# Attention with a soft mixture of experts: all transposes of an iteration in one run, and query loads of one iteration each

## The chip, the cores and the metric

The kernel runs on one core of a Trainium2 chip. The core has five engines with queues of their own: TensorE (PE; its weight loads are listed as PEld), VectorE (DVE), ScalarE (ACT), GpSimd (POOL) and SyncE (SP), which here only issues loads and stores; 16 DMA engines move the data. The metric is the device time of one execution in microseconds. Before the change three runs took 406.70, 407.28 and 407.36 us, median 407.28.

## The reference, cut to what matters

Three blocks follow one another, all in float32:

```
# attention: batch 4, 8 heads, 512 local and 32 global tokens, head size 64
s_g  = scale * q_g @ [k_g, k_l].T           ; out_g = softmax(s_g) @ [v_g, v_l]
s_l  = scale * q_l @ [k_g, k_l].T           # local keys only where |i - j| <= 32
out_l = softmax(s_l) @ [v_g, v_l]
x = [out_g, out_l] as 2176 x 512            # tokens of all batches, heads side by side
# soft mixture of 8 experts with 4 slots each
logits = x @ phi                            # 2176 x 32
d = softmax over the tokens ; slot_in = d.T @ x
slot_out = relu(slot_in @ w1[e]) @ w2[e]
y = softmax over the slots(logits) @ slot_out
# last block
h = y @ w_in ; out = (h - tanh(h)) @ w_out
```

## The kernel before, in words

The attention is a loop over `it` from 0 to 32. Iteration `it` handles block `it` of 32: a set s = it // 4 of one batch's four heads, and a quarter t = it % 4 of its tokens. It is software-pipelined: in iteration `it` the kernel computes the scores of block `it`, transposes the probabilities of block `it` - 1 and multiplies those of block `it` - 2 with v. Behind it, chains of small steps turn finished blocks into the input of the mixture. Engines work their queues in the order in which the code lists the instructions; waits between engines come from the data that they share. A tile of a pool with one buffer waits for the last reader of the tile before it.

In one iteration the steps that the change and the prediction speak of are listed in this order:

- `open_chains` (L625): the first half of each chain's present step (copies out of PSUM, exponentials), on ACT and DVE.
- `local_scores` (L236): TensorE's scores "sc" (L248) from the spread query `q_b[2]` and the keys, VectorE's masking (L254), ScalarE's exponentials (L258).
- `roll_k` (L218) and `spread_q(it + 1)` (L138) on GpSimd; both are copies by `pcopy` (L210). The spread overwrites the one `q_b[2]` tile, so it waits for the scores of this iteration, and the next scores wait for it.
- `local_transpose(it - 1)` (L265): four transposes "ptp" (L269) and a copy on ScalarE.
- `win_head` (L616) in every second iteration from 4 to 18: ScalarE's first step of turning float64 words of w_in into float32; the later steps run on VectorE in the next iteration.
- `local_values(it - 2)` (L274): "X" (L281); `global_values(it - 2)` (L467): "xgp" (L475), when t of that block is 0 or 1; `roll_v(it - 2)` (L223) on GpSimd, when t is 0, 1 or 2.
- `step_chains` (L630): the second half of each chain's step, in the order in which the chains were appended, all on TensorE. Among them are the transposes `turn_x` (L307, "xTp" L311, four), the two `turn` steps of `global_probs` (L449 four, L457 two), `turn` of `global_turn` (L494, one) and `turn` of `dispatch` (L379, one), and also steps that aren't transposes, `logits` (L339) and `gather` (L387).
- `global_probs` (L416) when it % 4 is 2: "gsc" (L430); then on GpSimd `spread_k` (L123) when t is 1 and `spread_v` (L127) when t is 3.
- SyncE: `load_q` (L132) in every second iteration, for the two blocks `it` + 4 and `it` + 5; loads of v when t is 2 or 3; then weights, as many KB as a pace (L724) allows; `load_qk` when t is 3. A load waits for the last reader of the place that it fills; that of a query waits for `spread_q(it + 1)`.

PSUM has eight banks: two for scores, one each for ptp, X, xgp and psL, two for psM. Before, psM held gsc, both turns of the global probabilities, xTp and the chains of `dispatch`, and psL held only the one transpose of `global_turn`.

After the loop (from L827) come the last X, the last logits, then the experts' weights (L971, L1010) and the last block.

Of the kernel before, what the change touches and what calls it, by code (L numbers as in the profile page):

```python
# [8 lines left out]
F32 = mybir.dt.float32  # L9
# [53 lines left out]
def band_attention_soft_moe_tanhshrink_kernel(  # L63
# [138 lines left out]
    NG = 4 * NST  # L202
# [103 lines left out]

    def turn_x(i):  # L307
        def transpose():
            ps = psM.tile([128, 512], F32, tag="m", name="xTp")
            for kc in range(4):  # L310
                T.transpose(ps[:, 128 * kc:128 * kc + 128], x_cols(i, 128 * kc, 128), ident)  # L311
            if i % 2 == 0:
                x2 = wk.tile([128, 2, 512], F32, tag="xT", name="xT", bufs=2)
                xT_t[i], xT_t[i + 1] = x2[:, 0, :], x2[:, 1, :]
            S.copy(out=xT_t[i], in_=ps)

        return [(None, transpose)]

# [6 lines left out]
    def dispatch(b, lbank=psm, tbank=psm, gbank=psm):  # L327
# [4 lines left out]
        st = {}  # L332
# [71 lines left out]
                    out=a, in0=a, scalar=f[rows], in1=st["s", cols.start][rows, cols], op0=ALU.mult, op1=ALU.add  # L404
                )

        chain = [(None, logits), (exps, turn), (turn_out, gather), (add, None)]
        return chain, dict(
            start=start, logits=logits, maxima=maxima, powers=powers, sums=sums, keep=keep, turn=turn,
            turn_out=turn_out, gather=gather, add=add,  # L410
# [5 lines left out]
    def global_probs(s):  # L416
        k, st = k_t[s], {}
        cuts = ((0, 512), (512, 576))

        def scores():  # L420
            for lo, hi in cuts:
                st[lo] = psM.tile([128, hi - lo], F32, tag="m", name="gsc")
            for lo, c, n, planes, groups in (
                (0, 0, 480, slice(0, 3), slice(0, 5)), (0, 480, 32, 3, 0), (512, 0, 64, slice(0, 2), 5),
            ):
                for i in range(2):
                    kn = k[:, i, planes, groups]
                    if n == 480:
                        kn = kn.rearrange("p q g c -> p g q c")
                    T.matmul(  # L430
                        st[lo][64 * i:64 * i + 64, c:c + n], lhsT=qg_t[s][:, 64 * i:64 * i + 64],
                        rhs=kn, skip_group_check=True, tile_position=(0, 64 * i),
                    )

        def exps():
            a = wk.tile([128, 4], F32, tag="gst", name="gst")
            for i, (lo, hi) in enumerate(cuts):
                V.tensor_reduce(out=a[:, i:i + 1], in_=st[lo], op=ALU.max, axis=AX.X)
            V.tensor_scalar(
                out=a[:, 2:3], in0=a[:, 0:1], scalar1=a[:, 1:2], scalar2=-0.125, op0=ALU.max, op1=ALU.mult  # L440
            )
            for o, i in (
                (pgl[:, 0:5, 0:96], st[0][:, 0:480].rearrange("p (i c) -> p i c", i=5)),
                (pgl[:, 0, 96:128], st[0][:, 480:512]),
                (pgl[:, 5, 0:64], st[512]),
            ):
                S.activation(out=o, in_=i, func=AF.Exp, scale=0.125, bias=a[:, 2:3])

        def turn():  # L449
            st["t"] = psM.tile([128, 512], F32, tag="m", name="gtp")  # L450
            for i in range(4):
                T.transpose(st["t"][:, 128 * i:128 * i + 128], pgl[:, i, :], ident)

        def turn_out():
            S.copy(out=gpt[:, 0:4].rearrange("p i c -> p (i c)"), in_=st["t"])

        def turn2():  # L457
            st["u"] = psM.tile([128, 256], F32, tag="m", name="gtp2")
            for i in range(2):
                T.transpose(st["u"][:, 128 * i:128 * i + 128], pgl[:, 4 + i, :], ident)  # L460

        def turn2_out():
            S.copy(out=gpt[:, 4:6].rearrange("p i c -> p (i c)"), in_=st["u"])

        return [(None, scores), (exps, None), (None, turn), (turn_out, turn2), (turn2_out, None)]

    def global_values(g):  # L467
        s, t = divmod(g, 4)
# [22 lines left out]
    def global_turn(b):  # L491
        st = {}

        def turn():  # L494
            st["p"] = psL.tile([128, 128], F32, tag="l", name="gxp")
            T.transpose(st["p"], gx_t.pop(b), ident)

        def turn_out():
            S.copy(out=xgT[:, :, b, :], in_=st["p"].rearrange("p (j q) -> p j q", j=4))

        return [(None, turn), (turn_out, None)]


    cool = []
# [120 lines left out]
    def open_chains():  # L625
        for c in chains:
            if c[0][0]:
                c[0][0]()

    def step_chains():  # L630
        for c in chains:
            if c[0][1]:
                c[0][1]()
        chains[:] = [c[1:] for c in chains if len(c) > 1]


# [3 lines left out]
    with tc.manual_schedule():  # L640
# [23 lines left out]
        for it in range(NG + 1):  # L664
# [8 lines left out]
                        spread_q(it + 1, (pcopy, pcopy))  # L673
            if 1 <= it < NG + 1:
                local_transpose(it - 1)
            free.extend(cool)
            cool.clear()
            if it < NG and it >= C0 and (it - C0) % 2 == 0 and (it - C0) // 2 < NIN:
# [7 lines left out]
                roll_v(it - 2)  # L686
            for f in last:
                f()
            step_chains()
            gs = (it + 2) // 4 if it % 4 == 2 and it + 2 < NG else 0 if it == 0 else None  # L690
            if gs is not None:
                c = global_probs(gs)
# [10 lines left out]
            i = it - 2  # L703
# [7 lines left out]
                spread_v(0)  # L711
            if it < NG and t == 3 and s < NST - 1:
                spread_v(s + 1)
            if it % 2 == 0 and it < NG - 4:
                load_q(it // 2 + 2)
            if it < NG:
                if it == NG - 5:
                    phi_g = ap_.tile([128, 192], F32, tag="qg", name="phi_g", bufs=1)
# [107 lines left out]

        dg["start"]()  # L827
        open_chains()
        values_last()
        step_chains()  # L830
        dg["logits"]()
        dg["maxima"]()
        last_turn(0)
# [670 lines left out]
```

## Time and profile before

| what | value |
|---|---|
| three runs | 406.70, 407.28, 407.36 us |
| the profiled execution's own time | 406.85 us |
| its span, first to last instruction | 405.1 us |
| mean granted TensorE clock | 0.993 of full speed |
| TensorE busy in the span | 382.9 us (95%) |
| VectorE, ScalarE, GpSimd busy | 276.2, 218.2, 209.7 us |
| bytes moved | 70.43 MB |
| the chain that ended last | PE 76%, issue 6%, POOL 5%, DVE 4%, DMA 3% |

"Busy" is the time in which an engine works on an instruction; matmuls are pipelined and overlap, so start-to-start distances say more of TensorE than durations do. In an answer of the trace, "[0.39 <-POOL q L210]" behind a row says that the engine stood idle for 0.39 us before it and what ended the idle time; "issue" means that the trace shows nothing that it waited for. One float32 matmul of the kernel gives several records, so the counts (x16, x32) are larger than the code's.

### The profile page before, as it was taken

To read this page: it belongs to the slowest core of one execution; us is meant where nothing else is said; L and a number is where in the kernel's file an instruction comes from. 1 tells how busy PE (TensorE), PEld (TensorE's weight loads), DVE (VectorE), ACT (ScalarE), POOL (GpSimd) and SP (SyncE) were. 2 spreads that over 40 slices of the span, in tenths; PEclk is the share of its full clock that TensorE was granted. 3 is DMA by queue.
4 is the path that set the end of the run, shared out by engine and by line. 5 is a ranking of instruction groups with operands and counts; after the bars stand their busy time and mean duration, and the time that the engine had idled before them with its cause. 6 is when DMAs were issued, how large, how long until landed. Compare 5 with 4: busy or idle time off the path is not lost.

```text
span 405.1 us, 10230 instructions
## 1 busy us (share of the span) xinstructions
PE 382.9 (95%) x3767; PEld 279.6 (69%) x3767; DVE 276.2 (68%) x833; ACT 218.2 (54%) x542; POOL 209.7 (52%) x275
## 2 busy tenths in 40 slices
PE   7889889989999899999999999999989999999994
PEld 3677667766787433336877786786868888888873
DVE  4577698766476526449998886787879997555541
ACT  2677666865766202248655645566575645345330
POOL 3676576665564010016866444455575668347441
PEclk9999999999999999999999999999999999999998
DMA  6899999999768989999303101003100003002104
GB/s 182 264 401 317 321 335 268 357 334 294 266 183 270 332 254 418 416 420 385 111 0 105 53 1 53 0 4 94 60 2 2 0 28 129 0 2 113 44 2 138
DMA packets 33834, 70.43 MB, mean 174 GB/s; under 512 B 3824, under 2 KB 10736, under 8 KB 33776
## 3 DMA queue, kind: packets, MB, share of 16 engines
q1 hardware_dynamic: 33632, 69.56, 50.3%
q8 instruction: 32, 0.52, 0.5%
q14 instruction: 26, 0.21, 0.2%
q10 hardware_dynamic: 144, 0.13, 0.1%
HBM read 65.22 MB, written 4.46 MB: 172 GB/s over the span
## 4 chain that ended last, share of the span: by engine, by line
PE 76%; issue 6%; POOL 5%; DVE 4%; DMA 3%; ACT 3%; SPq 2%; DVEq 0%; POOLq 0%
PE a L1175 13%; PE a L1176 13%; PE a L1174 13%; PE sc L248 7%; PE a L971 4%; PE a L1010 4%; PE h L1133 4%; PE X L281 3%; PE ptp L269 3%; SPq L104 2%; PE gsc L430 2%; POOL q L210 2%; PE xTp L311 2%; PE ps L344 1%; DVE slot L1150 1%
## 5 line engine op out<-in xcount | busy, mean ns | idle before, releaser
L1161 POOL TENSOR_TENSOR slot<-slot 128x384 fp32r<-128x384 f32 x96 | 98.7, 1031 | 83.5 <-ACT slot L1157 79.8
L1174 PE MATMUL a<-slot 128*128 128x512 f32 x272 | 106.9, 393 | 1.3 <-ACT v_w L1182 0.7
L1176 PE MATMUL a<-slot 128*128 128x512 f32 x272 | 107.8, 396 | 0.0
L1175 PE MATMUL a<-slot 128*128 128x512 f32 x272 | 107.5, 395 | 0.0
L1146 DVE SCALAR_TENSOR_TENSOR h<-slot,h 128x384 f32<-128x384 f32 x96 | 51.5, 537 | 38.7 <-ACT slot L1140 38.4
L1157 ACT CAST slot<-slot 128x384 fp32r<-128x384 f32 x96 | 47.6, 496 | 49.5 <-DVE slot L1150 49.0
L1140 ACT ACTIVATE slot<-h 128x384 f32<-128x384 f32 x96 | 45.3, 473 | 34.5 <-PE h L1133 33.9
L1174 PEld LDWEIGHTS a<-slot 128*128 128x128 f32 x272 | 51.1, 188 | 14.2 <-ACT v_w L1182 1.5
L1176 PEld LDWEIGHTS a<-slot 128*128 128x128 f32 x272 | 51.0, 188 | 11.4
L1175 PEld LDWEIGHTS a<-slot 128*128 128x128 f32 x272 | 51.0, 188 | 9.3 <-POOL slot L1037 1.0
L1150 DVE TENSOR_TENSOR slot<-slot,h 128x384 f32<-128x384 f32 x96 | 50.8, 529 | 8.0 <-DVE h L1146 0.5
L258 ACT ACTIVATE sm<-sm,mb 128x128 f32<-128x128 f32 x128 | 41.2, 396 | 15.5 <-DVE mb L254 15.2
L248 PE MATMUL sc<-k,q 128*64 128x128 f32 x512 | 39.0, 294 | 4.9 <-POOL q L210 3.8
L210 POOL TENSOR_SCALAR v<-v 32x1300 f32<-32x1300 f32 (+5 forms) x40 | 34.2, 855 | 13.9 <-PE xgp L475 11.4
L248 PEld LDWEIGHTS sc<-k,q 128*64 128x64 f32 x512 | 33.3, 208 | 11.1 <-POOL q L210 5.9
L210 POOL TENSOR_SCALAR q<-q 64x256 f32<-64x256 f32 x62 | 27.5, 444 | 20.5 <-issue 11.0
L254 DVE CUSTOM_DVE_ANT_0 sm<-sc,mask 128x128 f32<-128x128 f32 x128 | 30.2, 284 | 10.9 <-PE sc L248 9.7
L1037 POOL TENSOR_TENSOR slot<-k_w,slot 128x512 fp32r<-128x512 f32 x16 | 20.7, 1296 | 32.5 <-ACT slot L1036 32.3
L1133 PE MATMUL h<-slot 128*128 128x384 f32 x96 | 32.4, 339 | 0.8 <-DVE slot L1150 0.6
L1133 PEld LDWEIGHTS h<-slot 128*128 128x128 f32 x96 | 17.9, 188 | 12.0 <-DVE slot L1150 5.9
L281 PE MATMUL X<-v,pt 128*32 128x65 f32 x1024 | 22.1, 223 | 1.4 <-issue 1.4
L281 PEld LDWEIGHTS X<-v,pt 128*32 128x32 f32 x1024 | 16.5, 109 | 7.2 <-issue 6.1
(239 smaller groups left out, 526.2 us busy)
## 6 DMA issues: line engine op xcount, KB each, us to landing
slot<-in_w_dram SPq DMA_DIRECT2D x55, 512.0 KB, 7.6
slot<-in_w_out_dram SPq DMA_DIRECT2D x9, 512.0 KB, 4.8
slot<-in_w_in_dram SPq DMA_DIRECT2D x16, 256.0 KB, 6.5
k<-in_k_dram SPq DMA_DIRECT2D x7, 576.0 KB, 7.8
q<-in_q_dram SPq DMA_DIRECT2D x15, 256.0 KB, 5.4
out_dram<-o SPq DMA_DIRECT2D x15, 256.0 KB, 2.1
slot<-in_w_in_dram SPq DMA_DIRECT2D x7, 512.0 KB, 10.0
v<-in_v_dram SPq DMA_DIRECT2D x8, 390.0 KB, 5.5
```

The costliest lines, as they stand in the source:

```text
L210: G.tensor_scalar(out=o, in0=i, scalar1=0.0, scalar2=1.0, op0=ALU.add, op1=ALU.mult)
L248: T.matmul(sc[64 * i:64 * i + 64, a, :], lhsT=q_b[2][:, 256 * i + jj:256 * i + 256:4], rhs=k[:, i, :, WINDOWS[t][jj][0]], skip_group_check ...
L281: T.matmul(X[32 * jj:32 * jj + 32, h, :], lhsT=pt[:, 128 * jj + 32 * h:128 * jj + 32 * h + 32], rhs=v[:, WINDOWS[t][jj][0], 65 * h:65 * h ...
L1133: T.matmul(h, lhsT=mst(128 * fc, 128), rhs=cst(128 * t0 + c.start, n))
L1140: S.activation(out=u, in_=h, func=AF.Square)
L1146: V.scalar_tensor_tensor(out=h, in0=u, scalar=-2.5, in1=h, op0=ALU.add, op1=ALU.mult)
L1150: V.tensor_tensor(out=g, in0=u, in1=h, op=ALU.mult)
L1157: S.copy(out=ghi, in_=g)
L1161: G.tensor_tensor(out=glo, in0=g, in1=ghi.bitcast(F32), op=ALU.subtract)
L1174: T.matmul(acc_t[j], lhsT=ghi[:, c], rhs=whi[fc], start=first, stop=False)
L1175: T.matmul(acc_t[j], lhsT=ghi[:, c], rhs=wlo[fc], start=False, stop=False)
L1176: T.matmul(acc_t[j], lhsT=glo[:, c], rhs=whi[fc], start=False, stop=last)
```

## The change

All steps that are transposes get a third element "T" in their chain. `step_chains` takes an argument and runs twice per iteration: right behind `local_transpose` for the steps with "T", and at its old place for the others; only the second call advances the chains. The x transposes use psL (the one of tile 14 uses psM), and `global_turn` uses psM. `load_q` is called in every iteration, for block `it` + 5 alone (in iteration 0 for blocks 4 and 5), with 128 columns instead of 256.

```diff
     def turn_x(i):
         def transpose():
-            ps = psM.tile([128, 512], F32, tag="m", name="xTp")
+            pool, tag = (psM, "m") if i == 14 else (psL, "l")
+            ps = pool.tile([128, 512], F32, tag=tag, name="xTp")
...
-        return [(None, transpose)]
+        return [(None, transpose, "T")]
...
-        chain = [(None, logits), (exps, turn), (turn_out, gather), (add, None)]
+        chain = [(None, logits), (exps, turn, "T"), (turn_out, gather), (add, None)]
...
-        return [(None, scores), (exps, None), (None, turn), (turn_out, turn2), (turn2_out, None)]
+        return [(None, scores), (exps, None), (None, turn, "T"), (turn_out, turn2, "T"), (turn2_out, None)]
...
         def turn():
-            st["p"] = psL.tile([128, 128], F32, tag="l", name="gxp")
+            st["p"] = psM.tile([128, 128], F32, tag="m", name="gxp")
...
-        return [(None, turn), (turn_out, None)]
+        return [(None, turn, "T"), (turn_out, None)]
...
-    def step_chains():
+    def step_chains(turns):
         for c in chains:
-            if c[0][1]:
+            if c[0][1] and (len(c[0]) > 2) == turns:
                 c[0][1]()
+        if turns:
+            return
         chains[:] = [c[1:] for c in chains if len(c) > 1]
...
                 local_transpose(it - 1)
+            step_chains(True)
             free.extend(cool)
...
-            step_chains()
+            step_chains(False)
...
-            if it % 2 == 0 and it < NG - 4:
-                load_q(it // 2 + 2)
+            for g in (4, 5) if it == 0 else (it + 5,):
+                if g < NG:
+                    load_q(g // 2, slice(128 * (g % 2), 128 * (g % 2) + 128))
...
         open_chains()
+        step_chains(True)
         values_last()
-        step_chains()
+        step_chains(False)
```

## Rows read from the trace of the kernel before

**Rows 1.** Windows: busy us (and instructions) of each engine, granted clock, DMA share, GB/s.
```profile
core 0: us, PE busy (x) PEld busy (x) DVE busy (x) ACT busy (x) POOL busy (x), PEclk, DMA share, GB/s
20.00:100.00 80.00, 72.62 (x1558) 56.92 (x1548) 59.39 (x293) 55.44 (x158) 52.69 (x94) 1.00 0.99 328
100.00:124.00 24.00, 23.09 (x518) 18.61 (x520) 14.05 (x88) 17.78 (x52) 14.71 (x30) 1.00 0.73 236
140.00:160.00 20.00, 19.85 (x162) 6.29 (x161) 8.99 (x38) 2.23 (x7) 1.90 (x2) 0.91 0.92 325
```

**Rows 2.** Waits of TensorE, 8 to 132 us: total us, times, longest.
```profile
PE sc L248 <- POOL q L210: 3.8, 8, 1.0
```

**Rows 3.** TensorE's timeline, starts of scores: start us, us, instruction, idle before.
```profile
70.73 1.23 PE L248 MATMUL sc<-k,q 128*64 128x128 f32 x16 [0.39 <-POOL q L210]
...
81.71 1.23 PE L248 MATMUL sc<-k,q 128*64 128x128 f32 x16 [0.48 <-POOL q L210]
...
102.94 1.23 PE L248 MATMUL sc<-k,q 128*64 128x128 f32 x16
```

**Rows 4.** TensorE's timeline, stops without a releaser, first and last of seven.
```profile
20.83 0.32 PE L475 MATMUL xgp<-v,pg 128*32 128x65 f32 x7 [0.30 <-issue]
...
106.31 0.33 PE L460 MATMUL gtp<-ident,pg 128*128 128x128 f32 x1 [0.69 <-issue]
```

**Rows 5.** TensorE's timeline, groups in iterations 16 and 26.
```profile
68.55 0.67 PE L281 MATMUL X<-v,pt 128*32 128x65 f32 x32
69.14 0.66 PE L452 MATMUL gtp<-ident,pg 128*128 128x128 f32 x4
69.64 0.27 PE L496 MATMUL gxp<-ident,gx 128*128 128x128 f32 x1
69.75 0.60 PE L311 MATMUL xTp<-ident,x 128*128 128x128 f32 x4
...
108.16 0.66 PE L269 MATMUL ptp<-ident,sm 128*128 128x128 f32 x4
108.75 0.67 PE L281 MATMUL X<-v,pt 128*32 128x65 f32 x32
109.23 0.63 PE L475 MATMUL xgp<-v,pg 128*32 128x65 f32 x32
```

**Rows 6.** GpSimd's timeline, iterations 7, 10, 15 and 16, and 24.
```profile
36.19 1.63 POOL L210 TENSOR_SCALAR v<-v 32x1300 f32<-32x1300 f32 x1 [0.20 <-DMA v<-in_v_dram]
...
44.02 0.88 POOL L210 TENSOR_SCALAR q<-q 64x256 f32<-64x256 f32 x2
...
66.36 2.67 POOL L210 TENSOR_SCALAR v<-v 32x260 f32<-32x260 f32 x3 [0.39 <-PE xgp L475]
...
69.80 0.88 POOL L210 TENSOR_SCALAR q<-q 64x256 f32<-64x256 f32 x2
...
101.66 0.88 POOL L210 TENSOR_SCALAR q<-q 64x256 f32<-64x256 f32 x2
```

**Rows 7.** SyncE's timeline around the query load of iteration 10.
```profile
40.89 0.55 SPq L104 DMA_DIRECT2D slot<-in_w_dram  x1
44.92 0.55 SPq L104 DMA_DIRECT2D q<-in_q_dram  x1
```

**Rows 8.** DMA queue, 16:40 and then 160:180: packets, MB, share of 16 engines.
```profile
q1 hardware_dynamic: 5050, 8.39, 101.8%
...
q1 hardware_dynamic: 2290, 8.34, 102.2%
```

**Rows 9.** Tile v over the whole span: us from issue to landing of its loads.
```profile
DMA to landing us min/median/max: 2.6/5.1/8.0
```

**Rows 10.** Windows of TensorE alone: busy us, granted clock, DMA share, GB/s.
```profile
138.00:139.00 1.00, 0.36 (x8) 1.00 0.96 348
140.00:141.00 1.00, 0.85 (x7) 0.57 0.98 287
141.00:142.00 1.00, 1.00 (x8) 0.50 0.93 356
143.00:144.00 1.00, 1.00 (x12) 0.73 0.63 123
```

## The prediction before the result

> **What bounds the kernel now.** I read the windows first, then the waits and TensorE's timeline, then those of GpSimd and SyncE. The change touches only the 33 attention iterations (0 to 32), which run to about 131 us. There TensorE is busy 72.6 of 80 us, no other engine over 60, and the DMA engines are full (share 0.99) until 100 us and have room after it (0.73) [rows 1]. So an iteration mostly lasts as long as its TensorE queue: scores, the transposes of the probabilities, X, then whatever comes behind. Two things break this. The scores of some iterations (1, 2, 5, 6, 9, 14, 17 and 20 in the timeline) wait for GpSimd to spread their query, eight times, 3.8 us in all [rows 2, 3]. And TensorE stops seven times with no releaser that the trace shows, 0.30 to 1.38 us each, 5.6 us in all; the first and the last stand in [rows 4].
>
> **What joining the transposes saves.** Inside a run one transpose follows another after 0.11 us (69.64 to 69.75), but a lone group of four takes 0.59 us until the next kind starts (108.16 to 108.75) [rows 5]. So leaving a group costs 0.59 - 4 x 0.11 = 0.15 us. Before, an iteration leaves two groups, the probabilities' and the one behind the values; after, one: eight joined take 8 x 0.11 + 0.15 = 1.03 us against 2 x 0.59 = 1.18. That is 0.15 us per iteration that has a second group. What changes besides is the step out of X. X to a transpose takes 0.59 us, X to the global values 0.48 [rows 5]; X straight to the next scores, new in some iterations, has no row. I take 0.59, the row of X ahead of a wide weight load, so no gain; the other end is 0.11 us more in each of four iterations that TensorE sets, 0.4 us.
>
> By the flags, second groups stand in iterations 2, 4, 5, 7 to 10, 12, 13, 15 to 18, 20, 21, 23 to 26, 28, 29, 31 and 32: 23 of them, 3.4 us if TensorE set every iteration. It doesn't, so I go through them.
>
> **What a later X costs.** X and the global values start later in their iteration by the transposes now ahead of them, 0.44 us for a group of four. On GpSimd the roll of v waits for them; behind it stand, in every fourth iteration (3, 7, 11, ...), the spread of the next v, then the next iteration's roll of k and the query of the one after. In iteration 15 this chain starts with the v copies at 66.36 (2.67 us) and ends with the query at 69.80 + 0.88 = 70.68 [rows 6]; iteration 17 starts at 70.73 after waiting 0.39 us for it [rows 3]. There the 0.44 us lies on the path. In iteration 7 the spread of v waited for its load already (idle 0.20 us at 36.19) [rows 6]; a later roll fits in front of that, and only this iteration's own gain is lost. In iteration 23 the chain ends at 101.66 + 0.88 = 102.54 [rows 6] and iteration 25 starts at 102.94 [rows 3]: 0.35 us of slack after a hand-over of 0.05.
>
> **The ledger**, as the shift of the starts. Iteration 2: -0.15. 4 and 5 end in a wait for GpSimd, whose copies start from the scores: nothing. 7: lost at 9, still -0.15. 10: -0.30. 12: -0.45. 13: GpSimd again, nothing. 15: later by 0.44, so -0.01 at 17; 16 and 17 gain nothing, since GpSimd sets them. 18: -0.16. 20: -0.31. 21: -0.46. 23 and 24: GpSimd now ends at 102.54 - 0.46 + 0.44, so 25 starts at 102.57, -0.37. 25: -0.52. 26: -0.67. 28: -0.82. 29: -0.97. 31: -1.12. 32 gains 0.15 and gives back some 0.05, because fewer transposes are left between the X of block 30 and that of block 31, which needs v rolled in between. Sum: -1.2 us.
>
> **Banks and ScalarE.** The x transposes get the bank of psL to themselves, global_turn goes to psM. A group then has to wait for the copy of the iteration before, which ends before that iteration's successor has its scores: nothing. The copy of xT comes ahead of win_head on ScalarE, which makes VectorE's conversion in the next iteration up to 0.5 us later; it is placed behind the first scores there, and I count nothing. Uncovered, each would cost up to 0.5 us in iterations 8, 10, 16 and 18.
>
> **The query loads.** Those of the even iterations become half as large, and the odd ones get one each: 14 DMAs and 14 waits more on SyncE, each for the query spread of its own iteration. Behind such a wait stand the weight, v and k loads of that iteration. SyncE has room: its last load before the query of iteration 10 ended at 41.44, and the query left at 44.92 [rows 7], released by the spread that ended at 44.90 [rows 6]. Loads of odd iterations leave up to some 1.5 us later than now, while the engines have about 5 us of loads ahead of them. No query arrives later: half of them keep their iteration, half move one ahead. I count nothing; the other bound is rival 2.
>
> A row of a query becomes 512 B instead of 1 KB, which makes 15 x 256 = 3840 packets more. Two stretches with full engines price a packet [rows 8]: from 16 to 40 us 5050 packets (some 400 completion marks) take 101.8% of 16 x 24 us, 84 ns per data packet of 1.8 KB; from 160 to 180 us 2290 (some 250 marks) take 102.2% of 16 x 20 us, 160 ns per 4.1 KB. The line through both leaves 24 ns per packet at any size, so 3840 x 24 ns / 16 = 5.8 us of all engines; in proportion to bytes it would be 0. I take 5.8, and put it into the room from 100 to 124 us, 0.27 x 24 = 6.5 us. Loads with a deadline, v above all, land in 5.1 us in the median, 8.0 at most [rows 9], and are used some 2 us later than the median.
> On this the Trainium skill (DMA: Bandwidth & Descriptors, Specifications) has 512 B as the least size for line rate. By it the halves cost nothing and rival 2 loses its ground. The two stretches speak against it, but no row holds 512-byte queries alone.
>
> **After the attention.** From 140 us TensorE is busy again without a gap (19.85 of 20) [rows 1], on weights whose loads start when the attention frees their room; so that part moves forward with it, and the 1.2 us count whole.
>
> **Sum.** The profiled execution took 406.85 us: 405.65 after. The median of the runs stands 0.43 us above it, so for the median 406.1.
>
> **Rivals.**
> 1. No change: GpSimd takes the gain back. For it: it sets eight starts already, and the gains of 20 and 25 rest on the unexplained stops in them, which give GpSimd time. If iteration 7 pays 0.3 and 20 and 25 gain nothing, the sum is -1.2 + 0.3 + 0.3 = -0.6: 406.7. Against it: after iteration 20 no scores wait for GpSimd.
> 2. Slower: loads land late. The engines have 0.8 us free from 20 to 100 us, and some 4.9 of the 5.8 us fall there; at 100 us they would be 4 us behind, v's 2 us would be gone, and 2 us would come onto the path through the spread of v in iterations 19, 23 and 27: -1.2 + 2 = +0.8, 408.1. It decides from the point where v takes over 7 us to land. Against it: SyncE stands idle ahead of the query load [rows 7], so it isn't held up by loads that have not landed.
> 3. Slower: the clock. TensorE's granted clock fell to its lower level (0.50, 1.2 GHz) at about 140 us, after a thin stretch (0.36 of 1 us busy), and came back by 144 [rows 10]. Longer joined runs of transposes, up to 13, or a shifted end could bring another such fall. 3.3 us at half speed cost 1.65: -1.2 + 1.65, 407.7. Against it: it was 1.00 from 20 to 124 us [rows 1], with groups of four to nine in it.
> The Trainium skill (TensorE: Matmul & The Clock Gate, PE-mode transpose) says that transposes don't count as activity for this clock; longer runs of them would bring a fall nearer. No stretch of this trace shows one that a group caused.
> 4. The stops change. They are 5.6 us [rows 4]; a quarter more or fewer is 1.4 us either way. This sets the forecast's own width.
>
> **How the numbers follow.** Forecast 0.53, on its own 404.5 to 407.3 (the stops, and 0.4 for the step from X to scores); no change 0.24; loads late 0.15; clock 0.08. Under about 0.2%, 0.8 us, this measurement can't tell a change. Three quarters of the forecast lie below 406.5, and so does a third of rival 1 and the part of rivals 2 and 3 in which the stops shrink: faster 0.53, same 0.25, slower 0.22. The range 404.3 to 408.0 leaves out a little at both ends.
>
> **What would show it.** Right: transposes 0.11 us apart in one run, iteration 17 no earlier than 70.7, the scores of iteration 31 about 1 us earlier. Iteration 17 well ahead of 70.7 would prove the price of a later X wrong. Wrong altogether: GpSimd's waits for loads of v growing from iteration to iteration (rival 2), a granted clock below 1.00 before 135 us (rival 3), or stops that sum to over 2 us away from 5.6.

## The result, and the profile after

The changed kernel is slower: 408.84 us in the median of 20 runs, against 406.27 us in 20 runs of the kernel before. The ratio is 1.0068, with a 95% interval of 1.0045 to 1.0091, so 1.8 to 3.7 us. Medians are over all runs, ratios leave out runs more than 1.5% above the fastest of their kernel, so a ratio can differ from the quotient of two medians. The profiled execution took 408.66 us (span 406.8), 1.81 us more than that of before.

The windows that answer to [rows 1]; the last three numbers are granted clock, DMA share and GB/s:

```profile
20.00:100.00 80.00, 69.25 (x1481) 56.51 (x1470) 56.30 (x286) 53.66 (x150) 49.43 (x90) 0.98 1.02 318
100.00:124.00 24.00, 22.92 (x521) 19.28 (x523) 14.82 (x94) 18.32 (x56) 15.78 (x33) 1.00 0.90 267
```

The clock was 0.98 between 20 and 100 us, and the DMA engines, busier than before in both stretches, moved fewer bytes a second in the first (318 against 328 GB/s) and had to catch up in the second (267 against 236).

The waits of TensorE from 8 to 132 us (us in total, times, longest), the first row answering to [rows 2]:

```profile
PE sc L248 <- POOL q L210: 7.9, 8, 2.3
...
PE X L281 <- issue: 1.4, 1, 1.4
PE ps L345 <- issue: 0.9, 1, 0.9
```

The scores wait 7.9 us for GpSimd's query copies instead of 3.8, and the longest wait is 2.3 us instead of 1.0. The stops without a releaser, 5.6 us in seven before [rows 4], are two, 2.3 us in all. Not all of the rest is gone: the stop of 1.17 us in gsc behind iteration 10 stands in the changed kernel as a wait of 1.00 us for the load of k.

Where the time went, as start in the changed kernel minus start in the kernel before: scores of iteration 12 +0.37 us, of 13 +1.57, of 14 +2.61, of 17 +3.05 (73.78 against 70.73 in [rows 3]), of 20 +2.04, of 25 +2.10, of 31 +0.90; the first logits over the gathered rows, behind the loop, +2.16 (133.19 against 131.03). Smaller swings before it, +1.00 at 7 and +0.84 at 9, are mostly gone at 11. So there are two losses: 2.2 us around iteration 13, of which the later iterations give back the most (+3.05 at 17, +0.90 at 31), and 1.3 us between the last scores and those logits. One execution's starts are one sample: the runs of the kernel before spread from 402.7 to 409.1 us. I take the first loss first, along its chain. SyncE's timeline, iterations 7 and 10 (start, us, load), where that of before has the query load of iteration 10 at 44.92 [rows 7]:

```profile
37.95 1.41 SPq L104 DMA_DIRECT2D qg<-in_qg_dram  x1
...
46.58 0.55 SPq L104 DMA_DIRECT2D q<-in_q_dram  x1
47.44 0.34 SPq L104 DMA_DIRECT2D v<-in_vg_dram  x1
```

In the kernel before the group queries (qg) and the group values (vg) left at these places:

```profile
35.93 0.52 SPq L104 DMA_DIRECT2D qg<-in_qg_dram  x1
...
45.57 0.54 SPq L104 DMA_DIRECT2D v<-in_vg_dram  x1
```

GpSimd's timeline of the changed kernel, iterations 9 and 12:

```profile
44.88 0.51 POOL L210 TENSOR_SCALAR k<-qg 128x384 f32<-128x384 f32 x1 [1.75 <-DMA qg<-in_qg_dram]
...
54.73 1.27 POOL L210 TENSOR_SCALAR v<-v 32x1300 f32<-32x1300 f32 x1 [2.17 <-DMA v<-in_vg_dram]
56.08 0.40 POOL L210 TENSOR_SCALAR k<-k 128x256 f32<-128x256 f32 x1
56.45 0.88 POOL L210 TENSOR_SCALAR q<-q 64x256 f32<-64x256 f32 x2
```

And TensorE's, with the scores of iterations 13 and 14:

```profile
57.38 1.89 PE L248 MATMUL sc<-k,q 128*64 128x128 f32 x16 [2.29 <-POOL q L210]
...
61.56 1.23 PE L248 MATMUL sc<-k,q 128*64 128x128 f32 x16
```

The same two in the kernel before:

```profile
55.81 1.23 PE L248 MATMUL sc<-k,q 128*64 128x128 f32 x16
...
58.95 1.23 PE L248 MATMUL sc<-k,q 128*64 128x128 f32 x16 [0.25 <-POOL q L210]
```

TensorE's windows in the changed kernel around that wait (busy us, granted clock, DMA share, GB/s):

```profile
52.00:56.00 4.00, 2.89 (x78) 1.00 1.05 272
57.00:58.00 1.00, 0.62 (x7) 0.83 1.00 372
58.00:60.00 2.00, 2.00 (x16) 0.50 1.03 362
60.00:61.00 1.00, 1.00 (x9) 0.50 1.05 373
```

The group queries leave 2.02 us later than before. GpSimd's copy of them into k stands 1.75 us for them (0.69 before), the query copy behind it ends at 46.55 instead of 44.90, and SyncE's query load waits for that copy. So the group values behind it leave 1.87 us later, and 54.73 - 47.44 = 7.29 us pass until the spread that waits for them starts (the three loads of v at this place took 3.0 to 5.6 us to land before, 7.0 to 8.0 now). The spread of v stands 2.17 us for them; the roll of k and the query copy queue behind it, and the scores of iteration 13 stand 2.29 us. Then the granted clock falls to its lower level (0.50, 1.2 GHz): those scores take 1.89 us instead of 1.23, and iteration 13 lasts 61.56 - 57.38 = 4.18 us, 3.14 before. Of the 2.24 us between iterations 12 and 14, 1.20 come before the scores of 13 and 1.04 behind their start. Over the runs the mean granted clock is 0.988, against 0.992 to 0.993 in the sets of runs of the kernel before. The time lost at the lower level is (1 - clock) times the run: 4.9 us against some 3.1. That makes 1.8 of the 2.6 us, an estimate, and only if TensorE sets the time throughout.

The second loss, in TensorE's timeline after the scores of iteration 31:

```profile
125.60 1.23 PE L248 MATMUL sc<-k,q 128*64 128x128 f32 x16
...
129.99 0.33 PE L497 MATMUL gxp<-ident,gx 128*128 128x128 f32 x1 [0.69 <-DVE gx L487]
...
132.34 0.44 PE L312 MATMUL xTp<-ident,x 128*128 128x128 f32 x2 [0.61 <-DVE x L292]
...
133.19 1.04 PE L345 MATMUL ps<-xgT,phi_g 128*32 128x128 f32 x8
```

The first and the last of these in the kernel before:

```profile
124.70 1.23 PE L248 MATMUL sc<-k,q 128*64 128x128 f32 x16
...
131.03 1.06 PE L344 MATMUL ps<-xgT,phi_g 128*32 128x128 f32 x8
```

The transposes of gx and of the last x are now first in their iteration, ahead of the X that used to run while VectorE finished gx and x. From the scores to the logits it is 7.59 us; before, 131.03 - 124.70 = 6.33.

### The profile page after: what moved, and what is told of

Read it like the earlier page. It is cut to its first block, busy times and chain, and to the rows that moved or that the text cites. A ratio compares the mean times of both kernels' runs of the same rounds, so it can differ in the third digit from the quotient of the medians.

```text
span 406.8 us, 10253 instructions
## 1 busy us (share of the span) xinstructions
PE 379.9 (93%) x3767; PEld 281.0 (69%) x3767; DVE 274.6 (67%) x833; ACT 218.5 (54%) x542; POOL 207.9 (51%) x275
## 3 DMA queue, kind: packets, MB, share of 16 engines
q1 hardware_dynamic: 37440, 69.56, 51.8%
## 4 chain that ended last, share of the span: by engine, by line
## 5 line engine op out<-in xcount | busy, mean ns | idle before, releaser
L1152 DVE SCALAR_TENSOR_TENSOR h<-slot,h 128x384 f32<-128x384 f32 x96 | 51.6, 538 | 39.1 <-ACT slot L1146 38.9
L248 PE MATMUL sc<-k,q 128*64 128x128 f32 x512 | 40.0, 298 | 9.7 <-POOL q L210 7.9
L248 PEld LDWEIGHTS sc<-k,q 128*64 128x64 f32 x512 | 34.0, 208 | 15.1 <-POOL q L210 10.1
L254 DVE CUSTOM_DVE_ANT_0 sm<-sc,mask 128x128 f32<-128x128 f32 x128 | 30.1, 285 | 11.4 <-PE sc L248 11.4
L210 POOL TENSOR_SCALAR q<-q 64x256 f32<-64x256 f32 x62 | 26.3, 425 | 17.2 <-issue 8.6
L269 PE MATMUL ptp<-ident,sm 128*128 128x128 f32 x128 | 21.5, 291 | 0.6 <-ACT pt L271 0.6
```

The costliest lines, as they stand in the source:

```text
L210: G.tensor_scalar(out=o, in0=i, scalar1=0.0, scalar2=1.0, op0=ALU.add, op1=ALU.mult)
L248: T.matmul(sc[64 * i:64 * i + 64, a, :], lhsT=q_b[2][:, 256 * i + jj:256 * i + 256:4], rhs=k[:, i, :, WINDOWS[t][jj][0]], skip_group_check ...
L1152: V.scalar_tensor_tensor(out=h, in0=u, scalar=-2.5, in1=h, op0=ALU.add, op1=ALU.mult)
```

## The experiments

Each was timed in turn with the kernel before, on the same chip; "ratio" is to that kernel. Waits are those between 8 and 135 us, in one profiled execution of each kernel.

**The two parts alone.** q_only has only the last hunk of the loop's diff (`load_q` for one block an iteration); t_only has all the rest.

> The kernel before with the query loads of one iteration each alone; the transposes stand where they stood. Theory: the loss has two parts, about 1 us from query loads (512-byte rows and a wait of SyncE in odd iterations, so qg, k and vg land late and GpSimd hands over the query late) and about 1.3 us from the transposes of iterations 32 and after it, which now wait for VectorE. Then this kernel is 1 to 3 us slower than before (ratio 1.003 to 1.007), and GpSimd waits for the qg loads about 10 us in the attention, against 4.4 before, also with the old order of transposes. Rival, a later X alone delays GpSimd's roll of v: then this kernel is within 0.5 us of before and the waits for qg stay near 4.4 us.

> The change with the query loads of before: the order of the transposes alone. Theory: in the loop it gains about 1 us (0.15 us per group that TensorE sets), and the end loses 1.3 us (iteration 32 waits 0.7 us for gx and 0.6 us for x of VectorE): sum 0 to +0.5 us against before. Rival, a later X holds GpSimd up in every fourth iteration: slower by 2 us or more, with more than 3.8 us of scores waiting for GpSimd. The forecast of before the result would have 1.2 us faster.

q_only: 407.28 us, ratio 1.0036 (1.0003 to 1.0068). t_only: 405.37 us, 0.9989 (0.9960 to 1.0019). So the loads of one iteration cost something by themselves, and the joined transposes at most gain a little. The tail waits are in t_only too (0.70 and 0.61 us). GpSimd's waits for loads in q_only:

```profile
POOL k L210 <- DMA qg<-in_qg_dram: 10.6, 6, 2.1
POOL v L210 <- DMA v<-in_vg_dram: 2.0, 1, 2.0
```

Before, k waited 2.2 us for qg (4.4 over the whole span, the figure of the expectation) and v not at all for its group part. In q_only's trace the scores of iteration 9 stood 2.02 us for GpSimd, nearly as long as in the changed kernel, and yet the granted clock stayed at 1.00:

```profile
40.66 1.23 PE L248 MATMUL sc<-k,q 128*64 128x128 f32 x16 [2.02 <-POOL q L210]
```
```profile
36.00:46.00 10.00, 7.99 (x160) 1.00 1.05 311
```

**The end of the attention.** t_tail is t_only, and after_tail the changed kernel, with the old order in iteration 32 and behind the loop:

```diff
-            step_chains(True)
+            if it < NG:
+                step_chains(True)
...
+            if it == NG:
+                step_chains(True)
             step_chains(False)
...
         open_chains()
+        values_last()
         step_chains(True)
-        values_last()
         step_chains(False)
```

> As the order of the transposes alone, but in iteration 32 and behind the loop the transposes stand at their old places, behind X. Theory: the two waits for VectorE at the end are gone and 1.0 to 1.5 us come back against the kernel with the order alone, so 0.5 to 1.2 us faster than before. Rival (later X): the same time as the order alone, still slower than before.

> The changed kernel with its 512-byte query rows, but with the transposes of iteration 32 and behind the loop at their old places. Theory: the waits of the end for gx and x of VectorE, 1.3 us, go; from the scores of iteration 31 to the first logits of the global rows it takes 6.2 us instead of 7.6, and the kernel is 1 to 1.5 us faster than the changed one, so 1 to 2 us slower than before (ratio 1.002 to 1.005). Rival, the end is hidden behind the weight loads: ratio as the changed kernel, 1.007.

after_tail: 406.65 us, 0.9995 (0.9963 to 1.0027); t_tail: 405.40 us, 0.9977 (0.9946 to 1.0008). Both waits are gone from both traces, and scores to logits is 6.76 us in both, so 0.83 of the 1.26 us comes back. With the loads of one iteration this took the loss below what can be measured; between t_only and t_tail the runs show no difference, so they leave the size of this part open. Either repair alone, pair loads (t_only) or the old end (after_tail), takes the loss of about 3 us away, and both together (t_tail) take little more. So the parts measured alone, 1.5 us for the loads and -0.4 us for the rest, do not add up to the 2.8 us of the whole; the intervals are about as wide as the gap, and it was not tested why. t_tail has the lowest ratio of all, and its interval just reaches 1: it beats the changed kernel, and isn't shown to beat the one before.

**Row size against number of loads.** q_split issues each pair's load of the kernel before as two of 128 columns, both in the even iteration. The wide kernels lay the queries out in DRAM block by block, so that a load reads rows of 1 KB for one block and 2 KB for a pair: wide_after, wide_before, wide_t_tail and wide_split are the changed kernel, the one before, t_tail and q_split with that layout.

```diff
-                load_q(it // 2 + 2)
+                for half in range(2):
+                    load_q(it // 2 + 2, slice(128 * half, 128 * half + 128))
```

```diff
...
-            in_=qd[h // 2][:, :, 256 * (h % 2) + cols.start:256 * (h % 2) + cols.stop],
+            in_=qd[h // 2][:, 512 * (h % 2) + 2 * cols.start:512 * (h % 2) + 2 * cols.stop],
...
```

> The kernel before, where each load of a pair of query blocks is issued in the same even iteration as two loads of 128 columns: the 512-byte rows and the 15 more issues, without the waits of SyncE in odd iterations. If the rows are what costs (3840 packets of some 24 ns, 6 us of the 16 engines), it is as slow as the kernel with one-iteration loads, 1 to 3 us over before, with qg waits near 10 us. If the odd waits are what costs, it is within 0.7 us of before and the qg waits stay near 4 to 5 us.

> The changed kernel, but the queries lie in memory so that the 128 columns of both planes stand side by side for each block: a load of one block then has rows of 1 KB, as before the change, with the same odd waits and the same 30 loads. Theory, the 512-byte rows are the cost: it falls back by 2 to 3 us, to within 0.7 us of the kernel before (ratio 0.997 to 1.002), and the 16 engines' share of queue 1 until 135 us falls from 94% to about 90%. Rival, the waits of SyncE in odd iterations or the number of loads cost: it stays at 1.004 or more.

> The kernel before with the same layout: the loads of two blocks in even iterations have rows of 2 KB instead of 1 KB, half as many packets. Theory: the price of a packet works in this direction too, 1920 packets of 24 ns are 2.9 us of the 16 engines, and fewer loads land late: 0.5 to 2 us faster than before, with GpSimd's waits for qg under 3 us. Rival, before the change the loads were hidden with room: same time within 0.4 us.

> Joined transposes inside the loop, old order at its end, query loads of two blocks with rows of 2 KB: the best of both by the theory. 1 to 3 us faster than before (ratio 0.993 to 0.998). Rival, GpSimd sets the iterations anyway: no better than the kernel before with 2 KB rows alone.

> Each pair's query load issued as two loads in the even iteration, as in q_split (which was 3.0 us above the kernel before), but with the queries laid out so that each of the two reads rows of 1,024 bytes instead of 512. Theory (issues and their place, not rows): 2 to 3.5 us above the kernel before, as q_split. Rival B (512-byte rows): within 0.8 us of the kernel before.

q_split 408.88 us, 1.0075 (1.0041 to 1.0109); wide_after 409.51, 1.0052 (1.0008 to 1.0095); wide_before 405.53, 0.9993 (0.9961 to 1.0024); wide_t_tail 406.67, 0.9996 (0.9961 to 1.0030); wide_split 406.21, 1.0000 (0.9962 to 1.0038). Two loads instead of one cost as much as the whole change, with no move and no new order. Restoring 1 KB rows doesn't save the changed kernel (k still waits 8.0 us for qg), but it does save q_split: with two loads for a pair the rows cost some 3 us, and in the changed kernel no difference is shown, with an interval that leaves room for one. wide_after also shows what goes with a short or a long run: its five fastest had a clock of 0.992 to 0.999 and took 404.3 to 406.9 us, five others had 0.984 to 0.987 and took 409.1 to 410.3. (1 - clock) times the run, an estimate of the time lost at the lower level, is about 2 us for the first and 6 for the others, and their mean times lie 4.1 us apart.

**SyncE's order.** issue_only and issue_odd add to the kernel before loads that nobody needs; issue_only has one more of them, in iteration 0, and with it a load that overwrites its forerunner's tile at once.

```diff
+            if it % 2 and it < NG - 5:
+                load(out=extra[0:16, it // 2 % 2], in_=phid[0][0:16, 0, 0:4])
```

> The kernel before, its fifteen query loads and its order of transposes as they were, with 14 more loads of 16 rows of 16 bytes each into a tile that nobody reads, issued where the changed kernel issues its additional query loads. So SyncE has the additional issues, and neither the 512-byte rows nor the waits for GpSimd's copy of the odd iterations. Theory (the issues and what stands behind them on SyncE delay the key and value loads, and through GpSimd the scores): the time is 1.0 to 2.5 us above the kernel before, half or more of the 1.5 us that query loads of one iteration cost alone, PE's scores wait 5 to 7 us for the query copy (3.8 before). Rival A (the waits for the odd copies that stand in SyncE's order, not the issues): within 0.8 us of the kernel before, scores wait 3 to 5 us. Rival B (the DMA engines' time on the 512-byte rows): likewise within 0.8 us.

> The kernel before with 13 more loads of 16 rows of 16 bytes into a tile that nobody reads, in the odd iterations where the changed kernel issues its odd query loads; each overwrites the one before the last, so it has nothing to wait for on the chip (issue_only had one that stood 6.6 us behind its own forerunner and held SyncE that long). It leaves out nothing of the computation. Theory (issues on SyncE, about 0.55 us each, make the loads behind them late): 0.5 to 2 us above the kernel before, scores wait 5 to 7 us for the query copy. Rival (the wait of the odd query load for GpSimd's copy, or its rows, not the issue): within 0.6 us, scores wait 3 to 5 us.

issue_only: 414.40 us, 1.0208 (1.0157 to 1.0259), but its second load held SyncE for some 6 us, so it says nothing of issues. issue_odd: 408.73 us, 1.0077 (1.0043 to 1.0112), more than its theory allowed. Thirteen loads of 256 bytes, for which SyncE shows no wait, cost as much as the change does. GpSimd's wait at the spread of v (iteration 8), and the scores of iteration 9 behind it, in issue_odd:

```profile
38.31 1.28 POOL L211 TENSOR_SCALAR v<-v 32x1300 f32<-32x1300 f32 x1 [1.87 <-DMA v<-in_vg_dram]
```
```profile
40.98 1.23 PE L249 MATMUL sc<-k,q 128*64 128x128 f32 x16 [1.86 <-POOL q L211]
```

In its trace the clock then is 0.50 from 43 to 46 us, and again from 84 to 87, the second time behind a stop of 1.97 us in the scores of iteration 19, for which the trace names no releaser. The scores wait 5.5 us in all, as the theory had it.

q_behind_only is q_only with each odd load issued last in its iteration. t_tail_first is t_tail with the loads of v and qg issued ahead of the query load:

```diff
...
+            if it % 2 and it + 5 < NG:
+                load_q((it + 5) // 2, slice(0, 128))
```

```diff
+            if it < NG and t in (2, 3) and 1 <= s < NST - 1:
+                load_v(s + 1, t - 2)
+            if it < NG and t == 3 and s + 2 < NST:
+                load_qg(s + 2)
             if it % 2 == 0 and it < NG - 4:
                 load_q(it // 2 + 2)
...
```

> The kernel before with query loads of one iteration each, but each odd iteration's load issued last in its iteration, behind the value, weight and key loads; the order of transposes is as before. Theory (what stands behind the additional issue and its wait on SyncE is what is late): the group-query loads leave as early as in the kernel before, k waits for qg less than 5 us in all (10.6 us with the query load ahead, 2.2 before), and the time is 0 to 1 us above the kernel before (1.5 us with the query load ahead). Rival B (rows of 512 bytes, or more issues in all wherever they stand): 1.3 to 2.5 us above, as with the query load ahead.

> All transposes of an iteration joined except in the last iteration and behind it (t_tail, which was 0.9 us below the kernel before), query loads in pairs as before, and the value loads and the group-query load issued ahead of the iteration's query and weight loads. Theory (SyncE's order sets when GpSimd can spread, and so the scores): k waits for qg less than 2 us in all (4.6 us in t_tail), the scores wait 1 to 2 us less for the query copy, and the time is 1.5 to 2.5 us below the kernel before. Rival (the scores are held by GpSimd's own work whatever the loads do): 0.5 to 1.2 us below, as t_tail.

q_behind_only: 408.94 us, 1.0106 (1.0044 to 1.0168). Its k waits only 4.5 us for qg, as expected, and it is no faster for it: v waits 1.6 us for its group part. t_tail_first: 409.35 us, 1.0099 (1.0060 to 1.0139), missing its theory by over 5 us. Loads put ahead wait for the readers of their tile; SyncE stands 11.4 us for X, everything behind it leaves late, and the loads of v took 8.2 to 10.0 us to land between 28 and 44 us. Both refute the plain idea that an earlier place in SyncE's order is enough.

**The group values themselves.** late_v moves the loads of v and of its group part, in the kernel before, behind the weight loads. after_vg and after_tail_vg issue the group part of the changed kernel and of after_tail one iteration earlier:

```diff
-                if t in (2, 3) and 1 <= s < NST - 1:
-                    load_v(s + 1, t - 2)
...
+            if it < NG and t in (2, 3) and 1 <= s < NST - 1:
+                load_v(s + 1, t - 2)
             if it < NG and t == 3 and s + 2 < NST:
                 load_qk(s + 2)
```

```diff
...
+            if it < NG and t == 1 and 1 <= s < NST - 1:
+                load_vg(s + 1)
             if it < NG and t == 3 and s + 2 < NST:
                 load_qk(s + 2)
```

> The kernel before with one move: the loads of v and of its group part leave behind the weight loads of their iteration instead of ahead of them. Theory (a late group-value load is what costs: GpSimd's spread of v waits, the query copy behind it is late, TensorE's scores wait about 2 us and its granted clock falls): GpSimd's v waits for that load 2 to 6 us in all (nothing in the kernel before, 2.5 in the changed one), the scores wait 6 to 9 us for the query copy (3.8 before), and the time is 1.5 to 4 us above the kernel before. Rival (the late group-value load comes along with the loss but doesn't make it): within 0.8 us.

> The changed kernel with one move: the load of the group values leaves one iteration earlier, at the end of the iteration in which the tile's last readers are issued. Nothing else is moved. Theory: GpSimd's v no longer waits for that load (0 to 0.3 us in all; 2.5 in the changed kernel), no scores wait for more than 1.2 us, the granted clock stays at 1.00 from 8 to 135 us, and the time is 1 to 2 us below the changed kernel, so 0.6 to 1.6 us above the kernel before (the loss in the last iteration stays). Rival (the spread of v was not what cost): within 0.6 us of the changed kernel, 2 to 3.2 us above the kernel before.

> after_tail (the changed kernel with the old order in the last iteration, 0.6 us above the kernel before) with the group-value load one iteration earlier. Theory: both losses are gone, and what is left is the gain of joining against the other late loads: 0.3 to 1.3 us below the kernel before, clock 1.00 from 8 to 135 us. Rival: as after_tail, 0.3 to 1 us above the kernel before.

late_v: 416.73 us, 1.0256 (1.0203 to 1.0309), some 11 us, far over the 1.5 to 4 expected. Its waits on GpSimd, its waits on TensorE, and TensorE's windows at the two falls:

```profile
POOL v L210 <- DMA v<-in_vg_dram: 11.9, 4, 3.7
```
```profile
PE sc L248 <- POOL q L210: 14.9, 9, 3.0
```
```profile
56.00:64.00 8.00, 6.46 (x72) 0.57 1.00 320
77.00:81.00 4.00, 4.00 (x56) 0.57 1.07 330
```

So late loads of v are enough: in an otherwise unchanged kernel they give the waits and two falls of the clock, on a larger scale. Two things it leaves open. Its two longest waits for the query copy, 2.62 us at 95.03 and 3.05 at 112.78, had no fall behind them, so not every wait of this length brings one. And no run made v early in the changed kernel, so that v is what costs there is read from its trace.

after_vg: 407.70 us, 1.0054 (1.0021 to 1.0087); after_tail_vg: 407.17 us, 1.0027 (0.9990 to 1.0065). Neither gained. In after_vg the load left at 29.54 instead of 31.02 in the kernel before, but took at least 8.3 us to land (5.0 to 6.4 before), and GpSimd and TensorE show the same pair again:

```profile
37.96 1.27 POOL L213 TENSOR_SCALAR v<-v 32x1300 f32<-32x1300 f32 x1 [2.38 <-PE X L284]
```
```profile
40.61 1.99 PE L251 MATMUL sc<-k,q 128*64 128x128 f32 x16 [2.85 <-POOL q L213]
```

(The releaser named there, X, started at 37.10 and isn't read by the spread; I take the load for it, whose landing fits.) So it isn't the moment of issue alone; a longer queue ahead of the load would fit, but it wasn't measured.

**Another issuer.** after_tail_act and t_tail_act issue the loop's query loads from ScalarE:

```diff
...
-        DMA.dma_start(out=out, in_=in_)
+        (by or DMA).dma_start(out=out, in_=in_)
...
+            by=S if h > 1 else None,
...
```

> after_tail (the changed kernel with the old order in the last iteration, 0.6 us above the kernel before) with the query loads of the loop issued by ScalarE instead of SyncE, at the same place of each iteration. Theory S (the loads' issue and wait in SyncE's order is what delays the others): k waits less than 4 us for qg (7.6 us in after_tail), v not at all for its group load, the granted clock stays at 1.00 from 8 to 135 us, and the time is 0.5 to 1.5 us below the kernel before, against which ScalarE's 28 issues of about 0.55 us each, beside its waits for GpSimd's copies, may take back up to 1 us. Theory E (the engines deliver fewer bytes with more transfers in flight, whoever issues them): k waits 6 us or more for qg, the group load of v still lands 7 us or more after its issue, and the time is 0.5 to 1.5 us above the kernel before.

> t_tail (transposes joined except in the last iteration, queries in pairs; 0.8 us below the kernel before) with the query loads of the loop issued by ScalarE. Theory S: SyncE is freed of 13 issues and of its waits for GpSimd's copies, k's waits for qg fall from 4.6 us to under 2, and the time is 1 to 2 us below the kernel before. Theory E: within 0.5 us of t_tail.

after_tail_act 411.59 us, 1.0118 (1.0056 to 1.0180); t_tail_act 411.49 us, 1.0154 (1.0100 to 1.0208): 4.8 and 6.2 us above the kernel before, beyond both theories. Theory S falls: SyncE had lost the query loads, and k waited 9.9 us for qg in after_tail_act (7.6 in after_tail). In after_tail_act the loss isn't the chain above: v waited 0.2 us for its group part, and the profiled execution, 410.27 us, had a clock of 0.995. What makes it wasn't traced. In that trace the loads of v took, over the span:

```profile
DMA to landing us min/median/max: 3.3/6.9/10.6
```

after_tail had 2.7/5.7/8.7. The Trainium skill (DMA: Bandwidth & Descriptors, Queues, rings and completion order) says that an engine takes turns between its queues, a packet at a time; these landing times fit that, since with a second queue the first one's loads landed later.

**What stays open.** With more transfers v waited for its group part in most traces: 2.5 us in the changed kernel, 2.0 in q_only and after_tail, 1.9 in q_split and issue_odd, 1.1 in wide_split, 0.5 in wide_after, nothing before. Their number alone doesn't decide: wide_split has as many loads as q_split, with rows twice as long, and takes the time of the kernel before. By 38 us the kernel before had moved 287 GB/s x 38 us = 10.9 MB; the changed kernel 10.1 (267), wide_after 10.2 (269), issue_odd and wide_split 10.5 (277 and 276), t_tail 10.8 (285), with shares of 0.89 to 0.91 in all. So with more loads the engines delivered less in the same busy time. How much of that is a cost of each transfer or row in the engines and how much SyncE's later issues was not separated.

## Why the prediction was wrong

It forecast 406.1 us, 1.2 below the three runs that it knew (407.28), and 0.53 for faster. Measured are 408.84, above its range, against 406.27 in 20 runs of the kernel before.

- *"I count nothing"* for the query loads is the step that failed: the additional loads were taken to hide in SyncE's room. The room was read at one place [rows 7]. There the query load leaves 1.66 us later in the changed kernel, the group values behind it 1.87 us later, and the scores of iteration 13 stand 2.29 us. q_only has the loads alone at about 1.5 us (0.1 to 2.8), and issue_odd nearly as many transfers at 3.1 us without their bytes. That SyncE's room decides is not borne out either: in after_tail_act SyncE issues none of the loop's query loads, and the kernel is slower still.
- *The price per packet.* The count was off: 14 pairs are split, not 15, so 3,584 rows more. With 16 marks for each of the 14 more loads (issue_odd's 13 loads of 16 rows make 416 packets) that is 3,808, as q1 has (37,440 against 33,632). The 5.8 us of engine time were near by luck: q1 took 51.8% of 406.8 us, 7.0 us more than 50.3% of 405.1. But 3,968 fewer packets in wide_after leave 51.6% of 403.8, still 4.6 us more; issue_odd with 416 more than before has 51.3% of 406.9, 5.0 us more; and late_v with not one more has 50.6% of 414.7, 6.1 us more. So this time doesn't count packets. The Trainium skill (DMA: Bandwidth & Descriptors, Specifications) has 512 B as the least size for line rate; by it the shorter rows alone would cost nothing. q_split against wide_split (1.0075 against 1.0000) speaks against that here, and the changed kernel against wide_after shows no difference.
- *Rival 2*, chance 0.15, named the mechanism that the trace shows, the right load and, by luck, nearly the right time: its 408.1 adds a gain of 1.2 that no run shows and 2 us for v that were priced from another place. Its point, v taking over 7 us to land, was passed (7.29 us), but loads of v took up to 8.0 us before, too [rows 9], so that point told little. The 2 us that v was to have in hand were not there either: in iteration 7 the spread of v had waited for its load already, 0.20 us [rows 6]. Its places, iterations 19, 23 and 27 after a backlog that grows, were wrong: the worst wait came behind iteration 12, at 13; those at 9 and 25 were 1.12 and 0.54 us. What spoke against it, that SyncE wasn't held up by loads that hadn't landed, bears on the moment of issue and not on the landing.
- *Rival 3* had the clock falling by 1.65 us, but for long runs of transposes. The falls in the attention that were looked at, in the changed kernel, issue_odd, late_v and after_vg, come with scores ahead of which TensorE stood 1.9 to 2.9 us, not behind transposes. The reverse doesn't hold: q_only's 2.02 us and late_v's 2.62 and 3.05 us had no fall. The two rivals were priced as alternatives; in this trace the one follows the other.
- *Iteration 32* was to gain 0.15 and give back 0.05 us; it lost 1.26. The step looked at TensorE's queue and at v, and not at VectorE's gx and x, which the X ahead of the transposes used to hide.
- *A later X* costs 0.44 at iteration 17: its scores waited 1.12 us instead of 0.39, so 0.73. The 0.44 are there, the roll of v stands 0.83 us for the global values instead of 0.39 [rows 6]; the rest is the v copies, 2.99 us instead of 2.67. Iteration 25, priced at 0.09, waited 0.54.
- *Joining* itself was right in its mechanism: four kinds of transposes 0.11 us apart in one run, in TensorE's timeline of iteration 16.

```profile
70.42 0.65 PE L269 MATMUL ptp<-ident,sm 128*128 128x128 f32 x4
70.91 0.60 PE L453 MATMUL gtp<-ident,pg 128*128 128x128 f32 x4
71.35 0.27 PE L497 MATMUL gxp<-ident,gx 128*128 128x128 f32 x1
71.46 0.60 PE L312 MATMUL xTp<-ident,x 128*128 128x128 f32 x4
71.99 0.67 PE L281 MATMUL X<-v,pt 128*32 128x65 f32 x32
```

  Its worth, -1.2 us in the ledger, is not shown: against the kernel before, t_only lies at -1.6 to +0.8 us and t_tail at -2.2 to +0.3, which leaves room for -1.2 and for nothing.
- *The stops* moved by 3.3 us, more than the 2 us that the prediction allowed, 1.2 of them because the trace now puts the one in gsc down to the load of k. What makes them was not looked into.

## What to carry to other kernels

Where transfers feed a shared engine that spreads or rolls data, price an additional transfer by which load stands behind it and who waits in line for that load, not by its bytes or by the issuing engine's idle time at one place. A wait of 2 us of a busy TensorE costs more than 2 us where the granted clock falls behind it, which it did in some of these traces and not in others. When work is moved forward in a pipeline, look at the last iteration by itself: what was hidden by the next one's work has nothing to hide it there.

## What the runs showed of the hardware

Thirteen loads of 256 bytes made a kernel of 406 us slower by 3.1 us (1.7 to 4.5). Splitting 14 loads in two cost as much with rows of 512 bytes (q_split, 1.0075) and nothing measurable with rows of 1 KB (wide_split, 1.0000). Of two loads of the same group values, the one issued 1.5 us earlier (after_vg, 29.54 against 31.02) let the spread start 1.8 us later (37.96 against 36.19). A fall of the granted clock to 0.50 lasted 3 to 4 us in the changed kernel and in issue_odd, and nearly 7 us in after_vg. TensorE stood 2.29 us before the fall in the changed kernel; it stood 2.02 us in q_only and 3.05 us in late_v at a clock that stayed at 1.00.
